# A cached decode block on one core: the centred h as four row blocks, products without a reader in TensorE's waits, and the output weights in nine groups with six gathers

## The chip, the cores and the metric

One core of a Trainium2 chip runs the kernel as one program. Its engines are TensorE (PE; PEld is its weight load), VectorE (DVE), ScalarE (ACT), GpSimd (POOL) and SyncE (SP), and 16 DMA engines move data between the chip's main memory (HBM) and the on-chip buffers. The metric is the device time of one execution in microseconds (us); less is better.

## The reference

Two sequences with one new token each pass an attention block over a cache of 8192 positions and then a channel MLP. Everything is float32.

```python
# x (2,1,512); k, v (2,32,8192,128); wq (512,4096); wo (4096,512); w1 (512,1792); w2 (1792,512)
def _A_ref(x, k_cache, v_cache, wq, wo):            # H, Dh = 32, 128
    q = (x @ wq).reshape(B, Sq, H, Dh).transpose(0, 2, 1, 3)
    scores = jnp.einsum("bhqd,bhkd->bhqk", q, k_cache) * (Dh ** -0.5)
    o = jnp.einsum("bhqk,bhkd->bhqd", softmax(scores), v_cache)
    return o.transpose(0, 2, 1, 3).reshape(B, Sq, H * Dh) @ wo
def _B_ref(x, w1, b1, w2, b2):
    y = layernorm(x)
    return gelu(y @ w1 + b1) @ w2 + b2              # gelu: tanh form
h  = x + _A_ref(layernorm(x), k_cache, v_cache, wq, wo)
h2 = h + _B_ref(layernorm(h), w1, b1, w2, b2)       # _B_ref normalises again
```

## The kernel before

**Tiles and the loop.** The two caches are 537 MB, read once. They are cut into 32 K tiles and 32 V tiles of 8 MB, numbered 0 to 31: a tile holds two heads of one sequence, each head on 64 of the 128 partitions, 128 positions of 128 numbers on each partition (64 KB). Three buffers (pool `kv`, `BUFS = 3`) take the query weights, K and V tiles in turn, and at the end w1 and w2 together (`wt`). All these loads are issued by SP in program order: for step i, V tile i and then K tile i + 1. A load waits until the tile that last had its buffer is used up. Near the end K tile 29 is loaded in two parts, 30 in four, 31 in two, V tile 31 in four; V tile 30 and the last 256 rows of wo (`wl`) are queued behind K tile 31, and b1, b2, w1 (four parts) and w2 (six parts) behind V tile 31.

**One step.** For K tile i VectorE multiplies the tile by the query (`multiply`, L219, four chunks of 32 positions); the products are summed partly by VectorE (`by_dve`, L227) and partly by ScalarE (`by_act`, L223). `row_max` (L231, L234) and `all_max` (L238, L242) find the maximum, `exps` (L254) the exponentials, `values` (L279) multiplies them by V tile i on TensorE: 32 products of 512 columns per tile, `u` from 0 to 31, of which four go side by side into four column groups of one accumulator. (A float32 product stands as two MATMULs in the profile.) `gather` (L285) copies the accumulator, `head_sum` (L300; L293 for the last pair of heads) and `head_out` (L314) make the heads' outputs.

**The output weights.** All but the last 256 rows of wo are multiplied inside the loop, in groups: `load_wo` brings a group's rows to the buffer `wog` (one buffer), `turn` (L322) turns the matching head outputs, `turned` (L331) adds the products to `rowacc`, which begins as x. Before, there are eight groups of four rows per partition: the first four are gathers issued by POOL, which leave out the partitions of `SHUT` (0 to 7 and 32 to 39) and spread 448 rows over the other 112; the next four are plain loads of 512 rows issued by SP. Row places that are left out are zeros: POOL clears the buffer (L129) ahead of each gather (L130), and `orow`, two buffers of 2 rows taken by groups in turn, is zero there too. A group is loaded in the step after the one that used up the group before it. After the loop orow[0] becomes the bias tile `b1r`, cleared by a memset (L355) and filled by DMAs, and orow[1] holds b2 (`b2s`).

**The end.** While the last K tile is reduced, TensorE does the first 16 of V tile 30's products. Then, behind K tile 31's maximum: the other 16, V tile 31's 32 products, the last pair of heads (`head_end`, L293 and L422), and h less its mean: `base` is rowacc's copy, `basec` the same less its mean, `wlc` the last rows of wo less their means. The centred h is wanted with its 512 columns on the partitions, as four pairs of columns, `cen`. Before, it is made so directly: L484 uses 128 x 128 pieces of `wlc` as weights and the two head outputs as the moving side, eight products in all, and `basec` is turned by itself (L461) and added (L492). L489 adds the last heads to `po2`, which is seeded with h + b2 by L470. L501 multiplies `cen` by w1; L507, L509 and L511 make the scale of both layer norms from the squares of `cen`; L517 and L519 are bias and GELU, L521 a transposition; L524 multiplies by w2 into `po2`, L527 copies it, and two DMAs store it. `keep_warm` (L479) issues `WARM` products of the identity that nobody reads, between L501 and L524.

**What sets the order.** The framework keeps each engine's instructions in program order except where `behind(m)` puts an instruction behind m; waits between engines go through semaphores that it derives from the tiles. SP, POOL and each compute engine run their own queue in order.

Of the kernel before, what the change touches and what calls it, by code (L numbers as in the profile page):

```python
# [9 lines left out]
F32 = mybir.dt.float32  # L10
I32 = mybir.dt.int32
BF16 = mybir.dt.bfloat16
AF = mybir.ActivationFunctionType
ALU = mybir.AluOpType
AX = mybir.AxisListType

P = 128
EPS = 1e-5
QG = 2
# [1 line left out]
NACT = (13, 12, 12, 6)  # L21
BUFS = 3
NG = 4
WARM = 3
WR = 4

SHUT = [(0, 4, 32, 36)] * 4
FAR = 4096


# [1 line left out]
def tile_decode_block(ctx: ExitStack, tc: tile.TileContext, x, k, v, wq, wo, w1, b1, w2, b2, out):  # L32
    nc = tc.nc
    B, H, SK, DH = k.shape
    D = x.shape[-1]
    F = w1.shape[1]
    HP = P // QG
    NS = SK // HP
    NC = NS // CH
    DC = D // P  # L40
# [6 lines left out]
    const = ctx.enter_context(tc.tile_pool(name="const", bufs=1))  # L47
    wts = ctx.enter_context(tc.tile_pool(name="wts", bufs=1))
    kv = ctx.enter_context(tc.tile_pool(name="kv", bufs=BUFS))
    work = ctx.enter_context(tc.tile_pool(name="work", bufs=2))  # L50
    psq = ctx.enter_context(tc.tile_pool(name="psq", bufs=2, space=bass.MemoryType.PSUM))
    psm = ctx.enter_context(tc.tile_pool(name="psm", bufs=3, space=bass.MemoryType.PSUM))
# [18 lines left out]
    ident = const.tile([P, P], F32, name="ident")  # L71
# [9 lines left out]


    HL = H - QG
    GR = (P - 16) * WR
    groups = [(GR * g, GR, WR) for g in range(len(SHUT))]
    at = groups[-1][0] + GR
    while at < HL * DH:
        r = min(WR, (HL * DH - at) // P)
        groups.append((at, r * P, r))
        at += r * P  # L90
    kept = [[p for p in range(P) if g >= len(SHUT) or not any(s <= p < s + 4 for s in SHUT[g])]
            for g in range(len(groups))]
    group_end = {}
    for g, (r0, n, r) in enumerate(groups):
        group_end.setdefault((r0 + n - 1) // (QG * DH), []).append(g)

    part = const.tile([P, 1], F32, name="part")
# [1 line left out]
    next_of_pool(lambda: nc.gpsimd.iota(parti, [[0, 1]], base=0, channel_multiplier=1))  # L99
    nc.vector.tensor_copy(part, parti)  # L100
    index = {}
    for blocks in SHUT:
        if blocks not in index:
            acc = work.tile([P, 1], F32, name="ixf")
            nc.vector.tensor_copy(acc, part)
            for s0 in blocks:
                for edge, step in ((s0, FAR), (s0 + 4, -FAR - 4)):
                    one = work.tile([P, 1], F32, name="ix1")
                    nc.vector.tensor_scalar(one, part, edge - 0.5, float(step), op0=ALU.is_ge, op1=ALU.mult)
                    nc.vector.tensor_add(acc, acc, one)  # L110
            index[blocks] = const.tile([P, 1], I32, name="ix")
            nc.vector.tensor_copy(index[blocks], acc)
# [4 lines left out]
    wo_runs = wo.rearrange("(m r) n -> m (r n)", r=WR)  # L117
    wo_g = {}

    def load_wo(g, gate=None):  # L120
        r0, n, r = groups[g]
        t = wts.tile([P, WR, D], F32, name="wog")
        wo_g[g] = t
        if g >= len(SHUT):
            nc.sync.dma_start(t[:, :r], wo[r0:r0 + n, :].rearrange("(p r) n -> p r n", r=r))
            return
        if gate is not None:
            next_of_pool(lambda: nc.gpsimd.tensor_copy(gate0, gate))
        next_of_pool(lambda: nc.gpsimd.memset(t, 0.0))  # L129
        next_of_pool(lambda: nc.gpsimd.indirect_dma_start(  # L130
            t.rearrange("p r n -> p (r n)"), None, wo_runs, bass.IndirectOffsetOnAxis(index[SHUT[g]], 0),
            element_offset=r0 * D, bounds_check=P - 17, oob_is_err=False))

    epst = const.tile([P, 1], F32, name="epst")
    nc.vector.memset(epst, EPS)
# [24 lines left out]
    otl = const.tile([P, QG, B], F32, name="otl")  # L160
    sv = const.tile([P, 32], F32, name="sv")
    nc.vector.memset(sv, 0.0)
    so2 = [psa.tile([P, 512], F32, name=f"so{j}") for j in range(2)]
# [24 lines left out]
    for r in range(DC):  # L188
        for j in range(QW // 512):
            for n in range(NG):  # L190
                nc.tensor.matmul(so2[j][32 * n:32 * n + B], yT[:, r, :],  # L191
                                 wqt[:, r, n * QW + j * 512:n * QW + (j + 1) * 512],
                                 start=(r == 0), stop=(r == DC - 1))
# [3 lines left out]
    qps = {}  # L197
# [13 lines left out]
    ST, MX, MT, GM, LT, RL, SS, OP, TP = {}, {}, {}, {}, {}, {}, {}, {}, {}  # L211
    wl = q2.rearrange("p (e n) -> p e n", e=QG)
# [62 lines left out]
    def values(i, us=range(NS // 4)):  # L275
        so = so2[i % 2]
        for u in us:
            n = u % NG
            m = nc.tensor.matmul(so[32 * n:32 * n + 4 * QG], ptz[i % 2][:, u, :], vt[i][:, 4 * u:4 * u + 4, :],  # L279
                                 start=(u < NG), stop=(u >= NS // 4 - NG))  # L280
        return m

    def gather(i):
        SS[i] = work.tile([P, 512], F32, name="ss", bufs=3)
        return nc.scalar.activation(SS[i], so2[i % 2], AF.Copy)  # L285
# [17 lines left out]

    def head_out(h):
        rl = RL[h // QG * B + B - 1][:, h % QG:h % QG + 1]
        for g, (r0, n, r) in enumerate(groups):
            a, end = max(r0, h * DH), min(r0 + n, (h + 1) * DH)
            while a < end:
                q = (a - r0) // r
                run = 1  # L310
                while a + run * r < end and kept[g][q + run] == kept[g][q] + run:
                    run += 1
                c0, p0 = a - h * DH, kept[g][q]
                nc.vector.tensor_scalar(orow[g % 2][:B, :r, p0:p0 + run].rearrange("b r p -> b p r"),  # L314
                                        OP[h // QG][:, h % QG, c0:c0 + run * r].rearrange("b (p r) -> b p r", r=r),
                                        rl, None, op0=ALU.mult)
                a += run * r

    def turn(g):
        TP[g] = psm.tile([P, WR, B], F32, name="sm")  # L320
        for r in range(groups[g][2]):
            nc.tensor.transpose(TP[g][:, r, :], orow[g % 2][:B, r, :], ident[:B, :B])  # L322
        if g + 2 < len(SHUT) and SHUT[g + 2] != SHUT[g]:
            next_of_pool(lambda: nc.gpsimd.memset(orow[g % 2][:B], 0.0))

    def turned(g):
# [7 lines left out]
    def behind(m):  # L334
        return tc.issue_after(m.ins)
# [9 lines left out]
    for i in range(NI):  # L345
        m, b = divmod(i, B)
        done = i - 1
# [4 lines left out]
        else:  # L352
# [3 lines left out]
            b2s = rows2[:B, 1].rearrange("b r q -> b (r q)")  # L356
# [3 lines left out]
        if i > 0:  # L360
            last = all_max(done)
# [40 lines left out]
        if b == B - 1 and m + 1 < NM:  # L402
            make_q(m + 1)
        if late:
            with behind(values(done, range(NS // 8))):
                row_max(i)
        else:
            row_max(i)

    hl = NI - 1  # L410
    wt = kv.tile([P, 2, NS * DH // 2], F32, name="ws", tag="kv")
    w1t = wt[:, 0, :DC * F].rearrange("p (c f) -> p c f", c=DC)
    for c in range(DC):
        nc.sync.dma_start(w1t[:, c], w1.rearrange("(p c) f -> p c f", c=DC)[:, c])
    w2v = w2.rearrange("(p t) d -> p t d", t=FT)
    w2t = wt[:, 1, :FT * D].rearrange("p (t d) -> p t d", t=FT)
    for t, n in ((0, 4), (4, 4), (8, 2), (10, 2), (12, 1), (13, 1)):
# [2 lines left out]
    def head_end(i):  # L420
        head_sum(i)
        return nc.vector.tensor_tensor(otl[:, :, i % B], OP.pop(i), RL.pop(i), op=ALU.mult)  # L422

    last = all_max(hl)
# [3 lines left out]
        total(hl)  # L428
        ended = inverse(hl)
    with behind(last):  # L430
        last = values(hl - 1, range(NS // 8, NS // 4))
    gather(hl - 1)
    junk = const.tile([P, 2], F32, name="junk")
    nc.scalar.activation(junk[:, 0:1], LT[NM - 1][:, B - 1:B], AF.Sqrt)
# [6 lines left out]
    wlc = late[:, 0:QG, :]  # L441
# [9 lines left out]
    basec = late[:B, 3, :]  # L451
    nc.vector.tensor_scalar(basec, base, bmean, None, op0=ALU.subtract)
    nc.vector.tensor_add(b2s, base, b2s)

    with behind(last):
        first = values(hl, range(NS // 16))
    with behind(first):
        head_end(hl - 1)
    bcp = psm.tile([P, DC, B], F32, name="sm")
    for c in range(DC):  # L460
        last = nc.tensor.transpose(bcp[:, c, :], basec.rearrange("b (p c) -> b c p", c=DC)[:, c, :], ident[:B, :B])  # L461
    bct = const.tile([P, DC, B], F32, name="bct")
    nc.vector.tensor_copy(bct, bcp)
    po2 = psq.tile([P, 512], F32, name="po2", tag="qps")[:, :P]
    with behind(last):
        last = values(hl, range(NS // 16, NS // 4))
    gather(hl)
    with behind(last):
        for n in range(NG):
            last = nc.tensor.matmul(po2[32 * n:32 * n + 32], ident[:B, :32], b2s[:, n * P:(n + 1) * P],  # L470
                                    start=True, stop=False)
    with behind(last):
        head_end(hl)
    wb = ident.bitcast(BF16)
    wp = psq.tile([P, 512], F32, name="wp", tag="qps")[:, :2 * P]

    def keep_warm(n):
        for _ in range(n):
            nc.tensor.matmul(wp, wb[:, :P], wb, start=True, stop=True)  # L479

    acc = psm.tile([P, DC, B], F32, name="sm")
    for c in range(DC):
        for e in range(QG):
            last = nc.tensor.matmul(acc[:, c, :], wlc[:, e, :].rearrange("d (p c) -> d c p", c=DC)[:, c, :],  # L484
                                    otl[:, e, :], start=(e == 0), stop=(e == QG - 1))
    with behind(last):
        for n in range(NG):
            for e in range(QG):
                nc.tensor.matmul(po2[32 * n:32 * n + B], otl[:, e, :], wl[:, e, n * P:(n + 1) * P],  # L489
                                 start=False, stop=False)  # L490
    cen = const.tile([P, DC, B], F32, name="cen")
    nc.vector.tensor_tensor(cen, acc, bct, op=ALU.add)  # L492
    sq = const.tile([P, DC, B], F32, name="sq")
    nc.vector.tensor_tensor(sq, cen, cen, op=ALU.mult)
    nc.vector.tensor_reduce(sv[:, :B], sq.rearrange("p c b -> p b c"), axis=AX.X, op=ALU.add)
# [3 lines left out]
    for c in range(DC):  # L499
        for n in range(NG):  # L500
            last = nc.tensor.matmul(  # L501
                pf[32 * n:32 * n + B], cen[:, c, :], w1t[:, c, n * FN:(n + 1) * FN],
                start=(c == 0), stop=(c == DC - 1))
# [7 lines left out]
    nc.vector.reciprocal(rstd, std)  # L511
    nc.scalar.activation(junk[:, 1:2], std, AF.Gelu_apprx_tanh)
    with behind(last):
        keep_warm(WARM)

    gin = work.tile([P, FN], F32, name="gin", tag="ss", bufs=3)
    nc.vector.scalar_tensor_tensor(gin, pf, rstd, b1r, op0=ALU.mult, op1=ALU.add)  # L517
# [38 lines left out]
```

## Time and profile before

| | |
|---|---|
| Runs | 1313.37, 1315.71, 1316.23 us; median 1315.71 |
| Profiled execution | 1317.28 us, of which 1315.5 are the span of its instructions |
| Busy in the span | DVE 971.2 us (74%), ACT 479.4 (36%), PE 459.0 (35%), PEld 147.0 (11%), POOL 12.8 (1%) |
| DMA | 561.67 MB at 427 GB/s on average |
| Mean granted TensorE clock | 0.662 |
| Chain that ended last, by engine | DMA 44%, DVE 32%, PE 17%, issue 6%, ACT 1% |

The busy shares are means over stages with different limits. The chain is followed back from the last instruction: each piece is what released the next. "PEclk" is the share of full clock that TensorE was granted, in tenths in the slices. Lines such as L219 are lines of the kernel before.

### The profile page before, as it was taken

The page shows a single profiled execution, that of the slowest core. Times are in us where ns is not written, and L with a number is a line of the kernel's source. Part 1 is how long each engine was busy: PE and PEld are TensorE (multiplying, and loading weights), DVE is VectorE, ACT ScalarE, POOL GpSimd, SP SyncE. Part 2 cuts the span into 40 slices and gives each one's busy share as a digit, 9 for nine tenths or more (in the row PEclk, how much of TensorE's full clock was granted, in tenths as well). Part 3 has the DMA queues.
Part 4 walks back from the last instruction along what each step waited for, and adds up shares of the span by engine and source line. Part 5 has one row for each costly group of instructions (what it writes and reads, how often), then busy time and mean ns, then how long its engine had stood idle before and what let it go on. Part 6 is the DMA issues. An engine that isn't in the chain of part 4 may idle for free.

```text
span 1315.5 us, 10328 instructions
## 1 busy us (share of the span) xinstructions
PE 459.0 (35%) x3231; PEld 147.0 (11%) x3231; DVE 971.2 (74%) x447; ACT 479.4 (36%) x2955; POOL 12.8 (1%) x18
## 2 busy tenths in 40 slices
PE   3024213342332324313442332424412244323438
PEld 0001001110110101001010010101001011011104
DVE  1766788767788676788776788767688677798991
ACT  0333344433344333344333344333344333344441
POOL 0000000000000000000000000000000000000000
PEclk9566557766666667656766566766657676556758
DMA  9999999999999999999999999999999999999996
GB/s 415 443 417 441 422 439 439 423 437 430 433 435 425 439 431 429 431 430 437 431 427 437 435 427 435 425 439 435 425 437 430 435 433 425 439 423 423 442 415 263
DMA packets 13470, 561.67 MB, mean 427 GB/s; under 512 B 1556, under 2 KB 1572, under 8 KB 2984
## 3 DMA queue, kind: packets, MB, share of 16 engines
q1 hardware_dynamic: 12828, 557.34, 98.3%
q0 software_dynamic: 576, 3.67, 0.7%
q8 instruction: 25, 0.41, 0.1%
q14 instruction: 29, 0.24, 0.0%
q10 hardware_dynamic: 12, 0.01, 0.0%
HBM read 561.53 MB, written 0.00 MB: 427 GB/s over the span
## 4 chain that ended last, share of the span: by engine, by line
DMA 44%; DVE 32%; PE 17%; issue 6%; ACT 1%; POOL 0%; DVEq 0%; SPq 0%; POOLq 0%
DMA kv<-in_A_k_cache_dram 44%; DVE kv L219 21%; PE so L279 11%; DVE s L227 9%; PE rowacc L331 4%; ACT pt L254 1%; DVE orow L314 1%; PE so L501 0%; PE sm L242 0%; PE po L524 0%; PE sm L234 0%; DVE gm L238 0%; PE sm L484 0%; DVE mx L231 0%; ACT nb L248 0%
## 5 line engine op out<-in xcount | busy, mean ns | idle before, releaser
L219 DVE TENSOR_TENSOR kv<-kv,qps 128x4096 f32<-128x4096 f32 x128 | 560.7, 4411 | 277.5 <-DMA kv<-in_A_k_cache_dram 277.5
L223 ACT ACTIVATE kv<-kv 128x128 f32<-128x128 f32 x1376 | 403.9, 295 | 335.3 <-DVE kv L219 335.3
L227 DVE TENSOR_REDUCE s<-kv 128x20 f32<-128x2560 f32 (+2 forms) x128 | 377.7, 2972 | 0.3
L279 PE MATMUL so<-kv,pt 128*8 128x512 f32 x2048 | 284.3, 713 | 55.1 <-ACT pt L254 36.5
L223 ACT ACTIVATION_READ_ACCUMULATOR kv<-kv 128x1 f32 x1376 | 256.7, 187 | 0.0
L234 PE MATMUL sm<-ident,mx 128*1 128x128 f32 x32 | 11.1, 346 | 315.5 <-DVE mx L231 315.5
L285 ACT ACTIVATE ss<-so 128x512 f32<-128x512 f32 x32 | 19.1, 597 | 280.0 <-PE so L279 149.7
L204 PE MATMUL qps<-q,pick 2*64 2x128 f32 x128 | 16.7, 409 | 283.6 <-DVE kv L219 283.6
L279 PEld LDWEIGHTS so<-kv,pt 128*8 128x8 f32 x2048 | 58.3, 101 | 250.6 <-issue 208.7
L248 ACT ACTIVATE nb<-sm 128x1 f32<-128x1 f32 x32 | 5.5, 171 | 169.1 <-PE sm L242 169.1
L331 PE MATMUL rowacc<-wog,ot 128*2 128x512 f32 x64 | 47.4, 911 | 52.7 <-issue 27.1
L300 PE MATMUL sm<-ss,selr 128*2 128x128 f32 x480 | 55.8, 275 | 0.7 <-ACT ss L285 0.7
L204 PEld LDWEIGHTS qps<-q,pick 2*64 2x64 f32 x128 | 10.9, 202 | 297.4 <-DVE kv L219 274.4
L322 PE MATMUL sm<-ident,orow 2*128 2x2 f32 x32 | 4.5, 241 | 105.1 <-DVE orow L314 105.1
L300 PEld LDWEIGHTS sm<-ss,selr 128*2 128x2 f32 x480 | 39.2, 85 | 13.7 <-ACT ss L285 1.7
L234 PEld LDWEIGHTS sm<-ident,mx 128*1 128x1 f32 x32 | 2.5, 79 | 332.1 <-issue 287.5
L238 DVE TENSOR_REDUCE gm<-sm 1x2 f32<-1x128 f32 x32 | 8.9, 279 | 30.8 <-PE sm L234 30.8
L254 ACT ACTIVATE pt<-s,nb 64x128 f32<-64x128 f32 x64 | 25.5, 399 | 1.6 <-ACT nb L248 0.2
L331 PEld LDWEIGHTS rowacc<-wog,ot 128*2 128x2 f32 x64 | 6.6, 111 | 86.2 <-issue 60.3
L322 PEld LDWEIGHTS sm<-ident,orow 2*128 2x128 f32 x32 | 4.0, 209 | 107.3 <-issue 78.8
L242 PE MATMUL sm<-gm,srow 1*64 1x1 f32 x128 | 11.2, 238 | 11.5 <-DVE gm L238 11.5
L191 PE MATMUL so<-wqs,yT 128*2 128x512 f32 x64 | 9.2, 742 | 15.0 <-DMA wqs<-in_A_wq_dram 15.0
(100 smaller groups left out, 126.1 us busy)
## 6 DMA issues: line engine op xcount, KB each, us to landing
kv<-in_A_k_cache_dram SPq DMA_DIRECT2D x4, 4096.0 KB
kv<-in_A_k_cache_dram SPq DMA_DIRECT2D x4, 2048.0 KB, 26.5
wog<-in_A_wo_dram SPq DMA_DIRECT2D x4, 1024.0 KB, 36.3
kv<-in_A_v_cache_dram SPq DMA_DIRECT2D x1, 4096.0 KB, 36.0
ws<-in_B_w_dram SPq DMA_DIRECT2D x4, 896.0 KB, 10.8
kv<-in_A_v_cache_dram SPq DMA_DIRECT2D x1, 2048.0 KB, 40.5
ws<-in_B_w_dram SPq DMA_DIRECT2D x2, 1024.0 KB
kv<-in_A_v_cache_dram SPq DMA_DIRECT2D x1, 1536.0 KB
```

The costliest lines, as they stand in the source:

```text
L204: nc.tensor.matmul(qps[m][e * HP:(e + 1) * HP, b], pick[32 * n:32 * n + B, b, :], q2[32 * n:32 * n + B, at + e * DH:at + (e + 1) * DH], st ...
L219: return nc.vector.tensor_tensor(kc, kc, qb, op=ALU.mult)
L223: nc.scalar.activation(kt[i][:, j, :], kt[i][:, j, :], AF.Copy, accum_out=ST[i][:, j:j + 1])
L227: return nc.vector.tensor_reduce(ST[i][:, a:e], kt[i][:, a:e, :], axis=AX.X, op=ALU.add)
L234: nc.tensor.transpose(MT[i], mx, ident)
L242: nc.tensor.matmul(GM[i][e * HP:(e + 1) * HP], srow, gm[:, e:e + 1], start=True, stop=True)
L254: nc.scalar.activation(ptz[i % 2][ps, :, 4 * e:4 * e + 4], s[ps], AF.Exp, bias=nb[ps], scale=SCALE, accum_out=LT[m][ps, b:b + 1])
L279: m = nc.tensor.matmul(so[32 * n:32 * n + 4 * QG], ptz[i % 2][:, u, :], vt[i][:, 4 * u:4 * u + 4, :], start=(u < NG), stop=(u >= NS // 4 - ...
L285: return nc.scalar.activation(SS[i], so2[i % 2], AF.Copy)
L300: nc.tensor.matmul(OP[m][:, e, :], sel_row[:, c, 4 * e + j, :], SS[i - 1 + c][:, j * DH:(j + 1) * DH], start=(c == 0 and j == 0), stop=(c ...
L314: nc.vector.tensor_scalar(orow[g % 2][:B, :r, p0:p0 + run].rearrange("b r p -> b p r"), OP[h // QG][:, h % QG, c0:c0 + run * r].rearrange( ...
L331: nc.tensor.matmul(rowacc, t[:, r, :], wo_g[g][:, r, :], start=False, stop=(g == len(groups) - 1 and r == n - 1))
```

## The change

Three things change.

1. **wo's groups.** `PLAN` takes the place of `SHUT`: nine groups. The first is a plain load of one row per partition (128 rows), then six gathers of 448 rows, then two plain loads of 512 rows. The gathers leave out other blocks of four partitions: twice 0, 4, 32, 36; then 4, 12, 20, 36; 4, 24, 36, 68; 4, 36, 72, 76; and 80, 84, 88, 92. Each list has its own index tile. Where the list changes, POOL clears `orow` again.
2. **The centred h.** `hc` is a PSUM tile with four blocks of rows (0, 32, 64, 96), one for each 128 columns of h: `into` seeds it with `basec`, `project` adds the last heads with `wlc` as the moving side, a copy (`hs`) and one 128 x 128 transposition give `cen`. So `cen` goes by blocks of 128 columns, and w1 is loaded by blocks of 128 rows to match. `po2` is made by the same helpers.
3. **Order at the end.** 24 instead of 16 of V tile 30's products come before K tile 31's maximum (`MOST`). V tile 31's products go in four pieces that follow the four parts of its load, with 4 and 8 products without a reader between them, 4 behind them, and 16 in place of 3 behind w1's products. V tile 31's accumulator is copied half by ScalarE and half by VectorE.

In the program as built, `b1r`'s memset stands behind K tile 30's last reduction (nine groups end on orow[0]), the addition that makes `b2s` stands between `hs` and the copy to `cen` on VectorE, and on TensorE `po2`'s seed and products stand between `hc`'s products and the transposition.

```diff
--- before.py
+++ after.py
@@ -21,10 +21,12 @@
 NACT = (13, 12, 12, 6)
 BUFS = 3
 NG = 4
-WARM = 3
+WARM = 4
+MOST = 24
 WR = 4
 
-SHUT = [(0, 4, 32, 36)] * 4
+
+PLAN = [1, (0, 4, 32, 36), (0, 4, 32, 36), (4, 12, 20, 36), (4, 24, 36, 68), (4, 36, 72, 76), (80, 84, 88, 92), 4, 4]
 FAR = 4096
 
 
@@ -81,17 +83,17 @@
 
 
     HL = H - QG
-    GR = (P - 16) * WR
-    groups = [(GR * g, GR, WR) for g in range(len(SHUT))]
-    at = groups[-1][0] + GR
-    while at < HL * DH:
-        r = min(WR, (HL * DH - at) // P)
-        groups.append((at, r * P, r))
-        at += r * P
-    kept = [[p for p in range(P) if g >= len(SHUT) or not any(s <= p < s + 4 for s in SHUT[g])]
-            for g in range(len(groups))]
+    groups, at = [], 0
+    for blocks in PLAN:
+        shut = blocks if isinstance(blocks, tuple) else None
+        r = WR if shut else blocks
+        n = (P - 4 * len(shut or ())) * r
+        groups.append((at, n, r, shut))
+        at += n
+    assert at == HL * DH
+    kept = [[p for p in range(P) if not any(s0 <= p < s0 + 4 for s0 in shut or ())] for _, _, _, shut in groups]
     group_end = {}
-    for g, (r0, n, r) in enumerate(groups):
+    for g, (r0, n, r, _) in enumerate(groups):
         group_end.setdefault((r0 + n - 1) // (QG * DH), []).append(g)
 
...
@@ -118,18 +120,18 @@
     wo_g = {}
 
     def load_wo(g, gate=None):
-        r0, n, r = groups[g]
+        r0, n, r, shut = groups[g]
         t = wts.tile([P, WR, D], F32, name="wog")
         wo_g[g] = t
-        if g >= len(SHUT):
+        if not shut:
             nc.sync.dma_start(t[:, :r], wo[r0:r0 + n, :].rearrange("(p r) n -> p r n", r=r))
             return
         if gate is not None:
             next_of_pool(lambda: nc.gpsimd.tensor_copy(gate0, gate))
         next_of_pool(lambda: nc.gpsimd.memset(t, 0.0))
         next_of_pool(lambda: nc.gpsimd.indirect_dma_start(
-            t.rearrange("p r n -> p (r n)"), None, wo_runs, bass.IndirectOffsetOnAxis(index[SHUT[g]], 0),
-            element_offset=r0 * D, bounds_check=P - 17, oob_is_err=False))
+            t.rearrange("p r n -> p (r n)"), None, wo_runs, bass.IndirectOffsetOnAxis(index[shut], 0),
+            element_offset=r0 * D, bounds_check=n // r - 1, oob_is_err=False))
 
     epst = const.tile([P, 1], F32, name="epst")
     nc.vector.memset(epst, EPS)
...
@@ -320,7 +322,7 @@
         TP[g] = psm.tile([P, WR, B], F32, name="sm")
         for r in range(groups[g][2]):
             nc.tensor.transpose(TP[g][:, r, :], orow[g % 2][:B, r, :], ident[:B, :B])
-        if g + 2 < len(SHUT) and SHUT[g + 2] != SHUT[g]:
+        if g + 2 < len(groups) and groups[g + 2][3] and groups[g + 2][3] != groups[g][3]:
             next_of_pool(lambda: nc.gpsimd.memset(orow[g % 2][:B], 0.0))
 
     def turned(g):
@@ -402,7 +404,7 @@
         if b == B - 1 and m + 1 < NM:
             make_q(m + 1)
         if late:
-            with behind(values(done, range(NS // 8))):
+            with behind(values(done, range(MOST))):
                 row_max(i)
         else:
             row_max(i)
@@ -411,7 +413,7 @@
     wt = kv.tile([P, 2, NS * DH // 2], F32, name="ws", tag="kv")
     w1t = wt[:, 0, :DC * F].rearrange("p (c f) -> p c f", c=DC)
     for c in range(DC):
-        nc.sync.dma_start(w1t[:, c], w1.rearrange("(p c) f -> p c f", c=DC)[:, c])
+        nc.sync.dma_start(w1t[:, c], w1[c * P:(c + 1) * P])
     w2v = w2.rearrange("(p t) d -> p t d", t=FT)
     w2t = wt[:, 1, :FT * D].rearrange("p (t d) -> p t d", t=FT)
     for t, n in ((0, 4), (4, 4), (8, 2), (10, 2), (12, 1), (13, 1)):
@@ -428,7 +430,7 @@
         total(hl)
         ended = inverse(hl)
     with behind(last):
-        last = values(hl - 1, range(NS // 8, NS // 4))
+        last = values(hl - 1, range(MOST, NS // 4))
     gather(hl - 1)
     junk = const.tile([P, 2], F32, name="junk")
     nc.scalar.activation(junk[:, 0:1], LT[NM - 1][:, B - 1:B], AF.Sqrt)
@@ -452,44 +454,62 @@
     nc.vector.tensor_scalar(basec, base, bmean, None, op0=ALU.subtract)
     nc.vector.tensor_add(b2s, base, b2s)
 
-    with behind(last):
-        first = values(hl, range(NS // 16))
-    with behind(first):
-        head_end(hl - 1)
-    bcp = psm.tile([P, DC, B], F32, name="sm")
-    for c in range(DC):
-        last = nc.tensor.transpose(bcp[:, c, :], basec.rearrange("b (p c) -> b c p", c=DC)[:, c, :], ident[:B, :B])
-    bct = const.tile([P, DC, B], F32, name="bct")
-    nc.vector.tensor_copy(bct, bcp)
-    po2 = psq.tile([P, 512], F32, name="po2", tag="qps")[:, :P]
-    with behind(last):
-        last = values(hl, range(NS // 16, NS // 4))
-    gather(hl)
-    with behind(last):
-        for n in range(NG):
-            last = nc.tensor.matmul(po2[32 * n:32 * n + 32], ident[:B, :32], b2s[:, n * P:(n + 1) * P],
-                                    start=True, stop=False)
-    with behind(last):
-        head_end(hl)
     wb = ident.bitcast(BF16)
     wp = psq.tile([P, 512], F32, name="wp", tag="qps")[:, :2 * P]
 
     def keep_warm(n):
         for _ in range(n):
-            nc.tensor.matmul(wp, wb[:, :P], wb, start=True, stop=True)
-
-    acc = psm.tile([P, DC, B], F32, name="sm")
-    for c in range(DC):
-        for e in range(QG):
-            last = nc.tensor.matmul(acc[:, c, :], wlc[:, e, :].rearrange("d (p c) -> d c p", c=DC)[:, c, :],
-                                    otl[:, e, :], start=(e == 0), stop=(e == QG - 1))
-    with behind(last):
+            m = nc.tensor.matmul(wp, wb[:, :P], wb, start=True, stop=True)
+        return m
+
+
+    po2 = psq.tile([P, 512], F32, name="po2", tag="qps")[:, :P]
+    hc = psm.tile([P, P], F32, name="sm")
+
+    def into(t, rows):
+        for n in range(NG):
+            m = nc.tensor.matmul(t[32 * n:32 * n + 32], ident[:B, :32], rows[:, n * P:(n + 1) * P],
+                                 start=True, stop=False)
+        return m
+
+    def project(t, w, stop):
         for n in range(NG):
             for e in range(QG):
-                nc.tensor.matmul(po2[32 * n:32 * n + B], otl[:, e, :], wl[:, e, n * P:(n + 1) * P],
-                                 start=False, stop=False)
+                m = nc.tensor.matmul(t[32 * n:32 * n + B], otl[:, e, :], w[:, e, n * P:(n + 1) * P],
+                                     start=False, stop=stop and e == QG - 1)
+        return m
+
+    with behind(last):
+        last = values(hl, range(NS // 8))
+    with behind(last):
+        head_end(hl - 1)
+        last = keep_warm(WARM)
+    for a, e in ((16, 24), (24, 30), (30, 32)):
+        with behind(last):
+            last = values(hl, range(a, e))
+        if e == 24:
+            with behind(last):
+                into(po2, b2s)
+                last = into(hc, basec)
+            with behind(last):
+                last = keep_warm(2 * WARM)
+    SS[hl] = work.tile([P, 512], F32, name="ss", bufs=3)
+    nc.scalar.activation(SS[hl][:, :256], so2[hl % 2][:, :256], AF.Copy)
+    nc.vector.tensor_copy(SS[hl][:, 256:], so2[hl % 2][:, 256:])
+    with behind(last):
+        last = keep_warm(WARM)
+    with behind(last):
+        head_end(hl)
+        last = project(hc, wlc, True)
+    hs = const.tile([P, P], F32, name="hs")
+    nc.vector.tensor_copy(hs, hc)
+    with behind(last):
+        last = project(po2, wl, False)
+    hT = psm.tile([P, NG, 32], F32, name="sm")
+    with behind(last):
+        last = nc.tensor.transpose(hT.rearrange("p n r -> p (n r)"), hs, ident)
     cen = const.tile([P, DC, B], F32, name="cen")
-    nc.vector.tensor_tensor(cen, acc, bct, op=ALU.add)
+    nc.vector.tensor_copy(cen, hT[:, :, :B])
     sq = const.tile([P, DC, B], F32, name="sq")
     nc.vector.tensor_tensor(sq, cen, cen, op=ALU.mult)
     nc.vector.tensor_reduce(sv[:, :B], sq.rearrange("p c b -> p b c"), axis=AX.X, op=ALU.add)
@@ -511,7 +531,7 @@
     nc.vector.reciprocal(rstd, std)
     nc.scalar.activation(junk[:, 1:2], std, AF.Gelu_apprx_tanh)
     with behind(last):
-        keep_warm(WARM)
+        keep_warm(4 * WARM)
 
     gin = work.tile([P, FN], F32, name="gin", tag="ss", bufs=3)
     nc.vector.scalar_tensor_tensor(gin, pf, rstd, b1r, op0=ALU.mult, op1=ALU.add)
```

More of the change, by code (lines that the diff above doesn't have):

```diff
@@ L101, in tile_decode_block @@
     index = {}
-    for blocks in SHUT:
-        if blocks not in index:
+    for _, _, _, blocks in groups:
+        if blocks and blocks not in index:
             acc = work.tile([P, 1], F32, name="ixf")
@@ L305, in head_out @@
         rl = RL[h // QG * B + B - 1][:, h % QG:h % QG + 1]
-        for g, (r0, n, r) in enumerate(groups):
+        for g, (r0, n, r, _) in enumerate(groups):
             a, end = max(r0, h * DH), min(r0 + n, (h + 1) * DH)
```

## The prediction

> **What bounds it.** I read the page's slices first, then the waits, the chain that ended last, and for its end the timeline and stretches with their granted clock. In the slices, the DMA engines are full from the first to the last but one:
>
> ```profile
> DVE  1766788767788676788776788767688677798991
> PEclk9566557766666667656766566766657676556758
> DMA  9999999999999999999999999999999999999996
> ```
>
> The list of waits says who suffers: VectorE's multiply, 31 times, for a K tile.
>
> ```profile
> DVE kv L219 <- DMA kv<-in_A_k_cache_dram: 277.5, 31, 34.2
> ```
>
> So up to the last K tiles the time is bytes over the rate of the slowest of 16 engines. The chain shows where that ends (start, us, what):
>
> ```profile
> 1189.79 24.20 DMA kv<-in_A_k_cache_dram
> 1214.01 4.43 DVE kv L219
> ...
> 1281.94 3.54 PE so L279 x30
> 1285.48 0.98 PE sm L293 x8
> 1286.47 0.56 PE sm L461 x4
> 1287.03 5.31 PE so L279 x48
> 1292.37 0.60 ACT ss L285
> 1293.02 1.07 PE sm L293 x8
> 1294.32 3.90 PE sm L484 x16
> 1298.22 0.98 PE po L489 x16
> 1299.20 1.46 PE so L501 x6
> 1300.75 4.01 PE so L501 x24
> 1304.78 0.69 DVE gin L517
> 1305.50 0.97 ACT ff L519
> 1306.49 0.66 DVE pt L521
> 1307.20 4.95 PE po L524 x112
> ```
>
> The last wait for a load ends at 1214.01 (first quarter of K tile 30). Then VectorE is the chain until 1276.8, TensorE nearly to the end. In the stretches (us; busy PE, PEld, DVE, ACT, POOL; PEclk; DMA share, GB/s) the clock falls during L484 and is at half in most of L501 and L524:
>
> ```profile
> 1280.15:1297.21 17.06, 16.44 (x137) 8.02 (x129) 3.65 (x10) 3.19 (x7) 0.00 (x0) 1.00 0.96 382
> 1297.21:1304.04 6.83, 6.83 (x57) 2.85 (x60) 0.66 (x4) 1.75 (x3) 0.00 (x0) 0.50 0.99 404
> 1307.45:1310.87 3.42, 3.42 (x76) 2.62 (x68) 0.00 (x0) 0.00 (x0) 0.00 (x0) 0.50 0.02 5
> ```
>
> A second thread runs beside the chain: by the trace's sixteen completion marks of each transfer, the fourth part of w1 landed at 1298.75 and the last part of w2 at 1307.61. L501 and L524 came later anyway; if they come sooner, these landings decide.
>
> **wo: how the engines' loads shift.** Bytes stay. A 64 KB packet takes 2.42 us (median), so an engine left out of a whole gather (8 partitions of 8 KB) saves 2.42, half a gather 1.21. The completion marks show the lead of each engine over the last one. Before the gathers all lie within 0.8 us; after each, two engines (blocks 0/32 and 4/36) are about 2.4 further ahead. One of those two loses some 0.67 us at each of the 8 KB code reads that the trace has every 20 to 60 us, all on this one engine; eight or nine others lose some 1.55 us at a 16 KB code read, three times each; five lose nothing. When V tile 31 lands, the leads are 8.2 (the engine that also moves b2's row, so block 0/32), 6.0 to 6.7 (five), 1.7 to 3.2 (nine), and 0.0: the engine of the 8 KB reads, by elimination block 4/36. At 1214 the nearest is only 0.3 to 0.6 behind in lead.
>
> The new list, summed over direct groups too: block 0/32 gets 18 more pieces of 8 KB (0.302 us each), +5.4 us; 4/36 six fewer, -1.8; ten engines two fewer, -0.6; four two more, +0.6. New leads at the end: about 2.8, 1.8, 2.3 to 3.8, 5.4 to 6.1. The last engine finishes 1.8 sooner, and at 1214, where the others are nearest, 0.9 sooner (0.3 + 0.6). All gathers are out by the loop's 21st step (some 880 us), so both hold. Bounds: if the ten are not the engines that lag, the gain at 1214 is 0.3 - 0.6, thus a loss of 0.3; at the end -0.6 to +1.8. I take 0.9 and 1.8, since the shares removed are those the marks ask for.
>
> **Costs of the list that are covered.** Four more index lists (72 small VectorE operations at 0.15) fall into VectorE's 34 us of idleness before its first multiply. Two more gathers (L130 1.0 us, memset 1.8 each) and five memsets of orow are POOL's, 1% busy; the gathers read no more bytes, and a step with one was 2.49 us longer than one without against 2.48 with a direct load. The direct group of 128 rows is queued on SP behind a K tile, with a free buffer. With nine groups the last uses orow[0], so the 0.43 us memset of b1r (L355) moves behind K tile 30's last reduction; there VectorE idles 2.71 us for L238, because TensorE is in L331's rowacc until 1246.67. Covered by that; 0.43 if rowacc were quicker. b1's DMA behind it, and b2, w1, w2 behind that on SP, wait for completions much later than this.
>
> **The tail, by rows.** A "four" is four products side by side in column groups: 0.427 us for L279 at full clock, 0.854 at half.
> - V tile 30: 24 of its 32 products before K tile 31's maximum, not 16. The eight more are 4 fours, 1.7 to 3.4 us, beside VectorE's last reductions: the tile lands at 1268.2, 12 fours end by 1275.2 if the clock rises as late as two windows on, L234 needs TensorE at about 1276. This takes 1.7 us off TensorE's path behind L242.
> - L461 goes, -0.56; hc's seed (8 products like L470) comes, +0.35. Of the products without reader, 4 behind L293 and 8 behind the second part are on TensorE's path, since parts two and three have landed by then: 12 x 0.11 (L479's step) = +1.3.
> - So V tile 31's last product ends at 1292.3 - 0.9 - 1.7 - 0.56 + 0.35 + 1.3 = 1290.8; with the clock still half at the start of that stage I take 1291.0.
> - From there to L501, before: 6.65 (1292.30 to 1298.95). After: ACT's half copy 0.39 (0.60 for 512 columns, 0.17 for one); VectorE's half waits for it, the tile being one, but four of L293's eight run beside; L293 and its latency 1.1, otl 0.16, hc's 16 products 0.6 (as L489 at full clock), hs 0.29 (as L527). Then a queue order: VectorE has the b2s addition (0.68, as L453, off the path before) ahead of cen's copy, and TensorE has po2's seed, which waits for that addition, and po2's 16 products ahead of the transposition: 0.68 + 0.35 + 0.44, then 0.45, cen 0.17. With semaphores of 0.05: 4.9. So -1.75, though L484's 3.90 went. L501 starts at 1295.9.
> - L501: 5.76 now; at full clock 8 fours of 0.40 and L507: 3.45. L501's end to L524: 2.49, unchanged; the 16 products (13 more) lie in it, 1.75 at full clock, 3.4 at half. L524: 28 fours of 0.109 or 0.213, 3.3 or 6.2.
> - Full clock: L524 starts at 1301.8 and would end at 1305.1, 7.0 sooner; but w2's last part lands at 1305.8, then 2 fours and latency: 1306.4. L524 ended at 1312.1: **-5.7**, with the load deciding.
> - Loading w1 by blocks keeps rows of 7 KB (0.275 each): nothing.
>
> The clock: in the trace it changes in steps of 3.41 us. Windows that were dense raised it (1276.73 to 1280.15); one that was half full kept it (1187.98 to 1191.40); L484, mostly weight loads, lost it; 72% (1297.21 to 1300.62) did not raise it. After the change V tile 31's end, four products, L293 and hc's products fill some 45 to 60% of the window in question. I take full. Beside this: the Trainium skill, "TensorE: Matmul & The Clock Gate", Part 1, has half clock as the default, released after about one busy window of 3.4 us and taken back by an idle one, the windows running free of the kernel. By that rule alone L501 and L524 run full and the sum stays at -5.7; by the 72% row a lost clock comes back a window later than the rule would give it.
>
> The profiled execution took 1317.28 (span 1315.49 and 1.8 around), 1.6 over the median of 1315.71. Against it 1311.6; against the median 1310.0. Its cold tail may be part of why it is high, so I take the middle, **1310.8**.
>
> **Rivals.**
> - *The clock is lost as before.* For: a 1.3 us gap in TensorE before po2's seed, inside a window already thin. L501 5.76 and 16 cold products (+0.9): L524 starts at 1304.6 to 1305; full again, -4; half, -1.4. Time about 1313 (1311.7 to 1314.8). Chance 0.22.
> - *The relevelling does not take* (code reads fall a little otherwise): w2 lands at 1307.6 again, -3.9 and 0.9 of V tile 31's gain lost beneath it: 1312.6. Chance 0.14.
> - *Slower: the 8 KB code reads sit on another engine in the new program.* Some 24 reads x 0.67 = 16 us, now offset by four whole gathers (9.7). On an engine left out of half a gather it would end 16 - 1.2 - 6.5 = 8.3 us behind the present last one; loads decide as soon as that exceeds the 4 us by which L524 now comes late: 1307.6 + 8.3 + 0.6 is 4.4 later than 1312.1, and 1214 moves by as much as the reads until then. About 1321. Against: the same engine took them for 1200 us. Chance 0.09.
> - The forecast: 0.55.
>
> **Numbers.** A measurement here can tell about 0.2% (2.6 us): faster means under 1313.1. The forecast is nearly all under it, of the cold clock half, of the third case three quarters: 0.75; slower 0.09; the rest 0.16. The range leaves out the slower case and the cold one's end: 1307.8 (w2 another 2 us sooner, at the median) to 1314.8.
>
> **What would show it.** w2's last part landing at about 1305.8 and ending L524's wait; the 1214 wait ending near 1213; L478's hc products about 0.6 in place of 3.90; PEclk 1.00 across L501; a wait of po2's seed for the addition. Wrong if w2 lands after 1307.6, if PEclk is 0.5 through L501 and L524, or if V tile 31's products end after 1292.

## The result and the profile after

The changed kernel is slower: median 1371.52 us (1370.0 to 1372.68, four runs) against 1314.62 (1313.37 to 1316.23, four runs) before; the ratio is 1.043, 95% interval 1.0415 to 1.0445. The forecast was 1310.8 in a range of 1307.8 to 1314.8, and none of its rivals was this one.

The slices of the page of after (40 parts of 34.3 us) show first that the loads stop four times:

```profile
DVE  2777767880973967839678296788777678879892
DMA  9999999999599699996999969999999999999997
GB/s 425 429 431 431 427 434 431 438 437 428 222 427 434 266 431 444 438 423 253 429 429 434 444 251 429 433 446 427 431 433 431 429 438 433 434 421 427 442 417 283
```

The four weak slices lack 736 GB/s of 4 x 432: 736 / 432 x 34.3 = 58 us of full transfer, about all that was lost. The list of waits (who waited for what: us in total, times, longest) names a waiter that before did not have:

```profile
DVE kv L221 <- DMA kv<-in_A_k_cache_dram: 215.0, 23, 30.9
...
DVE ix L114 <- DMA wog<-in_A_wo_dram,ix: 113.9, 4, 28.8
```

L114 is the last operation of an index list, a cast of 128 numbers to integers (L112 before). It waits for a *gather*, that is, for a reader of the list before it. VectorE's timeline at the second of the four (start, length, instruction; in brackets the idle time ahead of it and what ended that):

```profile
404.12 0.28 DVE L240 TENSOR_REDUCE gm<-sm 1x2 f32<-1x128 f32 x1 [1.72 <-PE sm L236]
433.17 0.15 DVE L114 CAST ix<-ixf 128x1 int32<-128x1 f32 x1 [28.77 <-DMA wog<-in_A_wo_dram,ix]
...
435.18 8.75 DVE L221 TENSOR_TENSOR kv<-kv,qps 128x4096 f32<-128x4096 f32 x2
```

An operation of 0.15 us kept the engine idle for 28.77. The K tile multiplied at 435.18 had landed at 414.34 (completion marks), but its multiply was queued behind the cast. The Trainium skill, "Perfetto Trace Analysis", section "DVE / Act Engine Instruction (TENSOR_ADD, Activation, etc)", says that a slice begins only when the instruction executes and leaves the semaphore wait out. The row agrees: such a wait is found in the idle time ahead of an operation, not in its busy time (0.8 us for all five casts). The chain that ended last now runs through the gather:

```profile
403.96 1.80 POOL wog L131
406.02 27.13 DMA wog<-in_A_wo_dram,ix
435.18 8.75 DVE kv L221 x2
```

The DMA engines run dry later, since the loads already issued go on. Stretches behind the wait (busy PE, PEld, DVE, ACT, POOL; PEclk; DMA share, GB/s):

```profile
450.00:455.00 5.00, 0.00 (x0) 0.00 (x0) 5.00 (x2) 1.39 (x10) 0.00 (x0) 0.50 0.39 170
455.00:460.00 5.00, 1.12 (x8) 0.72 (x8) 5.00 (x2) 4.09 (x28) 0.00 (x0) 0.50 0.00 0
460.00:465.00 5.00, 0.30 (x1) 0.08 (x1) 4.45 (x3) 0.00 (x0) 0.00 (x0) 0.50 0.00 0
465.00:470.00 5.00, 3.33 (x21) 0.88 (x24) 4.89 (x3) 1.15 (x5) 0.00 (x0) 0.50 1.09 419
```

From 413.14 to 464.23 SP issued no tile load; the last load in flight landed at 454.92, so in the last 9 of these 51 us there was none, because no tile buffer came free while VectorE was late. The end of the kernel, where TensorE was the chain before, is now short of loads:

```profile
1303.18 40.48 DMA kv<-in_A_v_cache_dram
...
1353.07 13.57 DMA ws<-in_B_w_dram
1366.69 0.44 PE po L544 x8
```

**Why the cast waits.** All five lists are made by one line, `index[blocks] = const.tile([P, 1], I32, name="ix")`, in a pool with one buffer for each name. They are five tile objects with one name, so they share one buffer: a new list may be written only when the gathers that read the old one have landed. (The section on the change says that each list has its own index tile; that is true of the objects and not of the memory.) And although this code stands at the start of the source, the framework did not keep these casts there: in VectorE's order of the program as built, the first list stands ahead of the first multiply, and the other four casts stand inside the loop, each right ahead of a pair of multiplies. So the sentence in the description of the kernel that the framework keeps each engine's instructions in program order does not hold for these casts. The order could be read in the program as built before the run; the prediction takes all five lists to stand ahead of the first multiply.

### The profile page after: what moved, and what is told of

Read it like the earlier page. It is cut to its first block, busy times and chain, and to the rows that moved or that the text cites. A ratio compares the mean times of both kernels' runs of the same rounds, so it can differ in the third digit from the quotient of the medians.

```text
span 1370.6 us, 10503 instructions
## 1 busy us (share of the span) xinstructions
PE 455.4 (33%) x3268; PEld 143.4 (10%) x3268; DVE 980.1 (72%) x529; ACT 478.9 (35%) x2955; POOL 20.8 (2%) x26
## 4 chain that ended last, share of the span: by engine, by line
DMA 44%; DVE 36%; PE 10%; issue 8%; ACT 1%; POOL 1%; SPq 0%; DVEq 0%; POOLq 0%
DMA kv<-in_A_k_cache_dram 32%; DVE kv L221 23%; DVE s L229 11%; PE so L281 8%; DMA wog<-in_A_wo_dram,ix 8%; DMA kv<-in_A_v_cache_dram 3%; DMA ws<-in_B_w_dram 2%; PE rowacc L333 1%; ACT pt L256 1%; DVE orow L316 1%; POOL wog L131 1%; PE sm L236 0%; PE sm L244 0%; DVE gm L240 0%; DVE mx L233 0%
## 5 line engine op out<-in xcount | busy, mean ns | idle before, releaser
L221 DVE TENSOR_TENSOR kv<-kv,qps 128x4096 f32<-128x4096 f32 x128 | 560.7, 4411 | 215.0 <-DMA kv<-in_A_k_cache_dram 215.0
L114 DVE CAST ix<-ixf 128x1 int32<-128x1 f32 x5 | 0.8, 154 | 113.9 <-DMA wog<-in_A_wo_dram,ix 113.9
```

Source lines behind the costliest of these rows:

```text
L221: return nc.vector.tensor_tensor(kc, kc, qb, op=ALU.mult)
```

## The experiments

The theory: shared buffer, cast in VectorE's queue, multiplies behind it. The rivals: the two more gathers or the new sets of blocks hold up the loads; or the new end is slow. The kernel before, run beside each of them, had medians of 1315.6 to 1315.7, and ratios are against it. Its single runs lie mostly between 1313.2 and 1317.6, so a gain of 2 to 4 us is a matter of medians.

**Own buffers: `own_index`.** The whole edit:

```diff
-            index[blocks] = const.tile([P, 1], I32, name="ix")
+            index[blocks] = const.tile([P, 1], I32, name=f"ix{len(index)}")
```

> The changed kernel with a buffer of its own for each of the five index lists; nothing else. Theory 1, the shared buffer: in the trace of after the four later casts (L114) wait 113.9 us in all for gathers that still read the list before, VectorE's multiplies queue behind them, and the DMA slices fall to 222 to 266 GB/s four times. With own buffers the cast waits are gone, no slice before the last falls under 400 GB/s, and the time falls by some 55 to 62 us to the sum on record, about 1311 (1308 to 1315). Rival 2, the two more gathers or the new sets of blocks themselves hold up the loads: the dips stay, and the time stays above 1350. Rival 3, the new end of the kernel is slow: the dips go but the time stays above 1320.

Measured: 1311.66 (1311.39 to 1311.92), ratio 0.9968 (0.9952 to 0.9985): 0.3% under the kernel before, and far under the changed one. The casts all stand ahead of the first multiply, none waits, and the slices and the multiplies' wait are as before:

```profile
GB/s 417 433 431 427 434 433 437 437 425 432 429 447 421 437 431 435 427 439 429 433 435 435 430 431 437 427 432 429 441 425 441 425 438 429 428 429 430 434 425 322
```

```profile
DVE kv L221 <- DMA kv<-in_A_k_cache_dram: 271.0, 31, 27.2
```

So the whole loss, 59.9 us, was the buffer. The books agree: the casts waited 113.9, the multiplies 271.0 - 215.0 = 56.0 less, since VectorE would have waited for loads part of that time anyway; 57.9 is left, of a difference in span of 60.7. The rest fits the small operations themselves: behind the second and the third cast the 17 operations of a later list stand in the loop too (340.17 to 342.19 and 433.36 to 435.18, together 3.8).

**The list alone and the end alone.** `list_only` is the kernel before with the new `PLAN` and own index buffers. `tail_only` is the changed kernel with `PLAN = [(0, 4, 32, 36)] * 4 + [4] * 4`, the old list.

> The kernel before with only the new list of nine groups, each index list in a buffer of its own; the end of the kernel is the old one. Theory 1: no stall; the first quarter of K tile 30 lands about 0.9 us sooner and all behind it follows, so 0 to 2 us less than before: 1312.6 to 1314.6 (before: 1314.6). By the sum the landing of w2's last part goes 1.8 sooner, without effect here. Rival 2 (gathers or sets of blocks): above 1350 as in after. Rival 3 (the new end): as theory 1.

> The changed kernel with the old list (four gathers that leave out the same blocks, then four groups of 512 rows), so one index list; the new end of the kernel alone. Theory 1 and rival 2: TensorE's end comes 5 to 7 us sooner, and w2's last part, which lands where it did before (1307.6 in the trace), decides: 1310 to 1313, some 2 to 4 us less than before. Rival 3 (the new end is slow): above 1320.

Measured: 1313.39 (ratio 0.9985, 0.9974 to 0.9995) and 1312.76 (0.9985, 0.9976 to 0.9993). Neither is slow, so both rivals fall. Together they give 4.1, alone 2.3 and 3.0.

**One wait added to the kernel before: `one_shared`.**

```diff
-SHUT = [(0, 4, 32, 36)] * 4
+SHUT = [(0, 4, 32, 36)] * 2 + [(4, 0, 32, 36)] * 2
```

(`orow` is not cleared again, as the sets are the same.)

> The kernel before with a second index list in the same buffer for its third and fourth gather. The list holds the same four blocks in another order, so the gathers move the same rows through the same engines; what is added is one cast that has to wait for the first two gathers, and 18 small VectorE operations. Theory 1: one stall of 12 to 16 us (a quarter of what after lost), 1327 to 1331, with one slice near 250 GB/s and one L112 wait of about 28 us. Rivals 2 and 3: no difference, 1314 to 1316.

Measured: 1331.51, ratio 1.0128 (1.0109 to 1.0147), 15.8 us more, 0.5 above the top of what was expected. The same gathers, the same bytes; one wait and one weak slice, the ninth:

```profile
DVE ix L112 <- DMA wog<-in_A_wo_dram,ix: 28.5, 1, 28.5
```

```profile
GB/s 411 442 432 421 438 437 438 421 249 435 418 437 438 426 436 433 438 425 429 438 434 433 425 435 434 429 439 428 433 432 432 431 434 437 420 431 426 440 417 275
```

One wait costs 15.8 here and 15.0 in after (59.9 / 4).

**Two buffers in turn: `two_buffers`.** `name=f"ix{len(index) % 2}"`.

> The changed kernel with two buffers for the five index lists in turn, so that a cast waits for the gathers of the list before the last one, in place of the last one. Theory 1a, the place in VectorE's order is what costs: with two buffers the third, fourth and fifth cast still stand in VectorE's order right behind the gather that frees their buffer, far ahead of their use, so three waits of about 28 us and three stalls of some 15 us are left: 1311.7 + 45 = 1357 (1353 to 1361), three slices near 250 GB/s. Theory 1b, the lists only have to be a list apart: a gather is then long landed when its buffer is needed again, no wait, 1311 to 1313.

Measured: 1355.82, ratio 1.0315 (1.0299 to 1.0331). The usual cure of a second buffer saves one wait of four. Each list's turn comes a list earlier, and the cast still stands where its buffer comes free:

```profile
DVE ix L114 <- DMA wog<-in_A_wo_dram,ix: 85.2, 3, 28.8
```

44.2 us over own buffers is 14.7 a wait.

**The same buffer, the cast on another engine or elsewhere in the source: `cast_on_pool`, `cast_late`.** Both keep one index tile and cast just ahead of the first gather that uses the list; the float lists have buffers of their own. In `cast_late`, `nc.vector.tensor_copy(ix, index[shut])` stands in place of the added cast:

```diff
+        if cast != [shut]:
+            next_of_pool(lambda: nc.gpsimd.tensor_copy(ix, index[shut]))
+            cast[:] = [shut]
         next_of_pool(lambda: nc.gpsimd.memset(t, 0.0))
```

> The changed kernel with one index buffer as in after, but GpSimd makes the cast, just ahead of the first gather that uses the list; the float lists have buffers of their own. Each of the four casts still has to wait until the gathers of the list before have landed, but on GpSimd, with nothing but gathers and memsets queued behind. Theory 1 (what costs is the queue of multiplies behind the waiting cast on VectorE): 1311 to 1313 with no dip in the DMA slices. Against it (the shared buffer delays the gathers themselves, and these the kernel): stalls stay, above 1320.

> As the kernel with GpSimd's cast (one index buffer, float lists in buffers of their own, the cast written in the source just ahead of the first gather that uses the list, some 60 to 150 us behind the gather before), but the cast is made on VectorE again. In the program as built the four casts stand in VectorE's order right ahead of a pair of multiplies once more, and each waits for the gather of the list before. If that order is what costs: four waits of about 28 us and 1371 (1367 to 1374), as in after. If the place in the source decides, so that each cast comes when its gather has long landed: 1311 to 1313.

Measured: 1311.40 (ratio 0.9973, 0.9964 to 0.9982) on GpSimd, 1367.99 (1.0394, 1.0375 to 1.0412) on VectorE. One wait can be seen on GpSimd and costs nothing there (the other three casts, which were expected to wait as well, came after their gather had landed, since GpSimd had a memset of `orow` to wait for in between); on VectorE there are four again, and the casts stand at 340.9, 431.9, 603.9 and 775.3, within 3 us of after's, 64 to 146 us ahead of the gathers beside which the source has them:

```profile
POOL ix L133 <- DMA wog<-in_A_wo_dram,ix: 26.0, 1, 26.0
```

```profile
DVE ix L133 <- DMA wog<-in_A_wo_dram,ix: 113.3, 4, 28.9
```

So neither the sharing nor the wait is what costs, but what is queued behind the wait; and moving the line in the source does not move the instruction. `cast_late` is 3.5 us under the changed kernel; in it all the small operations stand ahead of the first multiply (the last at 14.8). Why the framework places the cast there was not tested.

**Six gathers with one list: `one_list`.** Own buffers, `PLAN = [1] + [(0, 4, 32, 36)] * 6 + [4, 4]`.

> The changed kernel with all six gathers leaving out the blocks 0, 4, 32 and 36, so that there is one index list and one cast. Theory 1: no stall in spite of six gathers; by the shares of the engines the first quarter of K tile 30 lands some 0.2 later than with the old list, so about 1.2 later than with own buffers (1213.7), and w2's last part about where it lands with own buffers (1305.5 to 1306.5): 1311 to 1313. Rival 2 (two more gathers hold up the loads): above 1320, with dips at the gathers.

Measured: 1312.98 (0.9988, 0.9979 to 0.9997). Six gathers cost nothing. The first quarter of K tile 30 landed at 1214.36 and w2's last part at 1307.59, 1.1 later than the top of what was expected: the shares of the engines were not known that well. The sets of the change are worth 1.3 us against it.

**No products without a reader: `no_extra`.** Own buffers, the four calls of `keep_warm` taken out.

> The changed kernel with own index buffers and without its 32 products without a reader; nothing else. If these hold the clock: PEclk 0.5 through L521 and L544, L521 about 5.8 in place of 3.8 and L544 about 6 in place of 3.4 without waits, so that TensorE's end passes the landing of w2's last part by about 1.4: 1312.5 to 1314, against 1311.7. If the other work holds it, or the landing decides anyway: 1311 to 1312.

Measured: 1311.63 (0.9975, 0.9966 to 0.9984), the same as with them. The clock was lower, 0.66 over w1's products (L516 here) against 1.00 in `own_index` (L521), and these took 4.89 in place of 3.79; yet it was back at 1.00 for w2's, and the landing of w2 decided anyway:

```profile
1293.67:1298.56 4.89, 4.86 (x40) 1.02 (x40) 0.48 (x3) 1.75 (x3) 0.00 (x0) 0.66 1.01 420
```

That the missing products lowered the clock is not shown. `cast_on_pool` has all 32 of them, and its clock over w1's products (L525 there) was as low:

```profile
1293.46:1298.30 4.84, 4.84 (x41) 1.08 (x42) 0.47 (x3) 1.75 (x3) 0.00 (x0) 0.66 1.01 421
```

Of the eight profiled kernels with the new end and the extra products, four had 1.00 over w1's products (`own_index`, `tail_only`, `one_list`, `cast_late`) and four less (the changed kernel and `cast_on_pool` 0.66, `level8` 0.79, `two_buffers` 0.59). In all eight the chain ends on w2's last part.

**A third list: `level8`.** Own buffers, `PLAN = [(4, 36, 12, 20)] * 2 + [(4, 36, 24, 68)] * 2 + [(4, 72, 76, 80)] * 2 + [(4, 84, 88, 92)] * 2 + [2]`.

> The changed kernel with own index buffers and a third list of nine groups: eight gathers of 448 rows, two each with the blocks 4, 36, 12, 20 left out, then 4, 36, 24, 68, then 4, 72, 76, 80, then 4, 84, 88, 92, and a last direct group of 256 rows. Against own index buffers alone, the engine of the 8 KB code reads moves 24 rows of 2 KB less (1.8 us by the 64 KB packet of 2.42), the ten middle engines 8 less (0.6), four 8 more (0.6), and the engine of the blocks 0 and 32, which here is left out no more, 72 more (5.4). If the slowest engines stand as the marks say (the first 0.6 behind nothing, nine with leads of 0.6 to 1.2) and the engine of 0 and 32 is the one with a lead of 7.0: w2's last part lands 0.6 to 1.2 sooner, 1304.8 to 1305.4, and the time is 1310.4 to 1311.1 against 1311.7. If that engine is one of those with 1.2 instead, it ends 4 later than the slowest does now: 1315 to 1316.

Measured: 1312.32 (0.9977, 0.9968 to 0.9986): a miss. K tile 30's first quarter did land 1.4 sooner than in `own_index` (1211.14), but w2's last part at the same 1305.97, so the time did not follow. The completion marks show where the gain went: when w1's last part landed (1295.94) the slowest engine was 0.16 behind the next, and when w2's first part did (1299.76) it was 1.33 behind. One 16 KB code read lies between the two, at 1297.6. `own_index` has one there as well (1297.7), but its slowest engine was 0.59 behind at w1's last part and 0.72 at w2's first. That the read fell on different engines would explain it, but the trace does not name the engine of a read, so it is not shown. What levelling can still bring here is of the size of such a read.

## Why the prediction was wrong, and where it was right

**The step that failed** is the first sentence of "Costs of the list that are covered": four more index lists "fall into VectorE's 34 us of idleness before its first multiply", and so cost nothing. The operations were counted rightly and are short; what they have to wait for, and where they stand, was not asked. The term is 59.9 us in place of 0: nearly all of it the waits; some 3.5, by the difference to `cast_late`, would be the operations of two lists that stand in the loop. Priced by the one wait that was added to the kernel before, it is 4 x 15.8, and the sum 1310.8 + 63.2 = 1374.0, against 1371.52 measured; by `cast_late` a wait is 14.1 ((1367.99 - 1311.66) / 4). No rival held it either: the slower one (code reads on another engine) was looked for among the DMA engines only, and nothing of it shows in `own_index`. The profile of before could not show this wait, since it has one list; the name of the tile and VectorE's built order could.

**The rest**, read from `own_index`, where the buffer is out of the way: 1311.66 for the profiled execution, and 1311.6 was the sum against the profiled one. The median is 1311.66 too, so the step from there down to 1310.8 was not borne out. Its chain and its timeline at the end:

```profile
1188.12 24.43 DMA kv<-in_A_k_cache_dram
1212.57 4.43 DVE kv L221
...
1282.80 9.44 DMA ws<-in_B_w_dram
1292.25 13.72 DMA ws<-in_B_w_dram
1306.01 0.44 PE po L544 x8
```

```profile
1290.62 0.64 PE L478 MATMUL sm<-late,otl 128*2 128x128 f32 x16 [0.25 <-DVE otl L424]
...
1291.56 0.67 DVE L455 TENSOR_TENSOR orow<-late,orow 2x512 f32<-2x512 f32 x1
1292.29 0.42 PE L471 MATMUL po<-orow,ident 2*32 2x128 f32 x8 [1.02 <-DVE orow L455]
...
1300.07 1.06 PE L544 MATMUL po<-ws,pt 128*2 128x128 f32 x32 [0.64 <-DVE pt L541]
```

- *Relevelling.* Taken as 0.9 at K tile 30's first quarter and 1.8 at w2's last part; these landed at 1212.55 and 1305.97, 1.4 and 1.6 sooner than before. Against `tail_only`, which has the old list (1213.54 and 1306.98), it is 1.0 and 1.0, so part of the first comparison's 1.6 is not the list's.
- *The other covered costs* were covered: gathers and memsets by `one_list` and `own_index`.
- *The tail.* V tile 31's last product ended at 1288.8, not 1291.0: in `tail_only` at 1290.4, where K tile 30 landed only 0.45 sooner than before, so some 1.5 of the difference to before's 1292.3 is not the loads', where the sum had 0.6; which term gave it stays open. From there to w1's products 4.97 against the 4.9 summed. The queue order that was foreseen is in the rows: the addition L455 and `po2`'s seed L471 ahead of the transposition, and `hc`'s products (L478) 0.64 in place of L484's 3.90. w1's products ended 3.79 after their start (3.43 busy, 3.45 by the sum, and a wait of 0.36 for w1's last part), and w2's began 2.49 later as said. They began at 1300.07 and not at 1301.8, and it made no difference: they waited for w2, as forecast, and ended at 1306.45 (1306.4 by the sum).
- *The clock* was 1.00 in all of this, as taken, but that was in part luck: four of the eight kernels with this end lost it for part of w1's products (see `no_extra`), where the prediction gave that a chance of 0.22. The price of that rival was wrong as well: about 1313, but `cast_on_pool`, at 0.66, took 1311.40. Its w1's products began at 1293.46, sooner than the 1295.9 of the sum, so that a slower stage still ended ahead of w2's landing. (The prediction's 72% for the window from 1297.21 to 1300.62 comes out only if the end of L484 is left out, 2.47 of 3.41 us; the row of the whole window has PE busy for 3.41.)
- *The rival without relevelling* was put at 1312.6; `tail_only`, which is that case, took 1312.76, though w2's last part landed there at 1306.98 and not at 1307.6.

## What to carry to other kernels

A new tile under an old name is a wait on all readers of the old one: when a change makes a small tile several times, look at the pool's buffers and at where each write stands in the built order of its engine, to the last one. Price a wait not by the instruction but by what is queued behind it on an engine that runs in order: 28 us on VectorE cost 15 each time, 26 on GpSimd nothing. If the tiles are small, give each its own buffer; neither a second buffer nor moving the line in the source was enough.

## What was not expected of the hardware

A gather of 448 rows of 2 KB takes 26.1 to 27.1 us from issue to landing while the tile loads keep the DMA engines full. By the fit for GpSimd's DMAs in the Trainium skill ("DMA: Bandwidth & Descriptors", section "Anatomy of one DMA — SWDGE (gpsimd) path", 2.0 us plus bytes over 436 GB/s) an estimate would be 4.1; the measurement decides. The fit has no term for what is queued on the engines already; no run here has a gather beside idle engines, so that this is the reason is not shown. And three tile buffers carried the DMA engines about 20 us past the landing of the gather (433 to 452) before they ran dry; how much of a stall is lost depends on what is in flight, not on the wait's length alone.
